# Static attention scores as four quarter-array products of 192 columns, and one PSUM tile per bank

## The chip, the cores and the metric

The kernel runs on one core of a Trainium2 chip. The metric is the device time of one execution in microseconds; a lower time is better. A core has five engines with queues of their own: TensorE (PE; its weight loads are PEld), VectorE (DVE), ScalarE (ACT), GpSimd (POOL) and SyncE (SP), which here only issues DMA transfers. TensorE writes its products to PSUM, eight banks of 512 fp32 columns on 128 partitions; VectorE and ScalarE fetch them from there.

## The reference

Block-sparse attention for 4 batches, 8 heads, 768 positions and a head dimension of 64, and behind it an MLP on the 3072 tokens (width 512, hidden 2048). The mask is by blocks of 32: each query block sees its own and its two neighbours, the first and the last block, and three sampled blocks.

```python
scores = scale * np.matmul(q, k.transpose(0, 1, 3, 2))
mask = np.abs(blk_i - blk_j) <= 1
mask = mask | (blk_i == 0) | (blk_j == 0) | (blk_i == n_blocks - 1) | (blk_j == n_blocks - 1)
for qb in range(n_blocks):
    for kb in sampled_blocks[qb]:
        mask[qb * 32:(qb + 1) * 32, kb * 32:(kb + 1) * 32] = True
scores = np.where(mask, scores, -1000000000.0)
attn = np.exp(scores - np.max(scores, axis=-1, keepdims=True))
attn = attn / (np.sum(attn, axis=-1, keepdims=True) + 1e-09)
x = np.matmul(attn, v)                      # then tokens x 512
h = x @ w_in
r = np.maximum(h, 0.0)
out = (s * (r * r) + b) @ w_out
```

The weights of the MLP come in as float64 and are turned on the chip into two fp32r parts each (high and low).

## The kernel before

**Slots and units.** The attention is a list of slots. A slot of kind s is one batch, one tile of 128 queries and four heads, so four units (one unit is one head's 128 x 352 scores); there are 40. Kind d (dense: the first and the last query block, eight slots of two units with 768 keys each) and kind h (four slots, the queries left over) handle the edges. The query tiles are shifted by one block, so that tile t holds the query blocks 4t+1 to 4t+4.

**One unit's columns.** A unit of kind s has 352 score columns in one bank: 256 static ones (128 of its own chunk of keys, 64 of the first and last block, 64 of the next chunk) and 96 sampled ones. The static scores are one product per head (L710): 64 partitions of head dimension, 128 queries as weights, 256 key columns. Two heads share a call: one sits on array rows 0 to 63, the other on 64 to 127 (`tile_position`). Query blocks 4t+1 and 4t+2 need only columns 0 to 191 of the 256, blocks 4t+3 and 4t+4 only columns 64 to 255; the mask adds a very large negative number to the others. The sampled scores (L736) are 32-query products with gathered keys. Slots d and h (L724) already multiply 64 queries at a time, by four products per call on the four quarters of the array, 384 and 160 columns wide.

**A unit's way.** VectorE adds the mask and takes the maximum (L751, with the scores read from PSUM into an SBUF tile), ScalarE takes the exponential and the row sum (L763), TensorE transposes 3 x 128 columns into another bank (L787), VectorE or ScalarE in turn copies them out (L791, L793), TensorE multiplies with the static values (L832) and the gathered ones (L846). Per slot follow the reciprocal of the sums (L772 to L775), the scaling (L852), a transposition (L858), a copy (L863) and a DMA to DRAM.

**Banks.** `next_bank` goes round seven banks for scores and transposed tiles alike; each call makes a new tile under the bank's tag, which waits until the tile before it under that tag is done. The eighth bank holds the attention's output.

**Order.** No engine's order is left to a scheduler of the compiler. The class `Plan` simulates five queues (TensorE, ScalarE, VectorE, GpSimd, SyncE) with a cost in nanoseconds for each operation (`costs` at L956 for TensorE's, others beside the operation), a priority, and counts of buffers; each engine takes, when free, the operation of best priority that can start first. The order that comes out is the order of the program. TensorE's own order is fixed before that: transposes of slot i, the transposition of slot i-1, the scores of slot i+2, the products with values of slot i. Into the same plan go the decoding of the weights (L75 to L85: six VectorE and three ScalarE operations for each of 32 blocks, with three raw buffers), at a lower priority than the attention, and the first 30 of the 64 steps of the MLP for batches 0 and 1 (`mlp1`, L401 to L403, then ReLU, square, high and low part, `mlp2`, L440 to L442). Behind the plan stand, in an order written out by hand, the rest of those steps and the MLP of batches 2 and 3 (L1193 and on), which uses seven products for eight.

**Limits at the passage.** The hidden tiles have two buffers, their high parts three, and `mlp1` two banks; so `mlp2` of the first step has to run before the fourth step's hidden tile can be finished. `mlp2` of step 0 needs w_out block 0 decoded; the order of decode is w_in blocks 0 to 7, then w_out 0 and so on.

Of the kernel before, what the change touches and what calls it, by code (L numbers as in the profile page):

```python
# [15 lines left out]
ALU = mybir.AluOpType  # L16
# [82 lines left out]
class Plan:  # L99
# [103 lines left out]
def kernel(  # L203
# [16 lines left out]
    nc = tc.nc  # L220
# [3 lines left out]
    D = 64  # L224
# [6 lines left out]
    SC = 256  # L231
# [28 lines left out]
    NBANK = 7  # L260
# [12 lines left out]
    def bank(k, name):  # L273
        return ps.tile([P, 512], F32, tag=f"bank{k}", name=name)
# [184 lines left out]
    with ExitStack() as es:  # L459
# [66 lines left out]
        for t in ptiles:  # L526
            nc.gpsimd.memset(t[:, SW:], 0.0)

        V = nc.vector
        ri = pers.tile([P, 1], I32, name="ri")  # L530
        V.tensor_scalar(out=ri, in0=pi, scalar1=5, scalar2=None, op0=ALU.logical_shift_right)
# [162 lines left out]
        bcount = [0]  # L694

        def next_bank(name):
            bcount[0] += 1
            return bank(bcount[0] % NBANK, name)

        halves = [slice(par * D, (par + 1) * D) for par in range(2)]  # L700

        def scores_static(i, k):


            kind, b, t, x = slots[i]
            n, qr, kt = unit_of[i], qraw[slots[i][:3]], kts[b]
            if kind == "s":
                for par in range(2):
                    sp = sps[(n + 2 * k + par, 0)] = next_bank(f"s{n + 2 * k + par}")
                    nc.tensor.matmul(sp[:, :SC], qr[halves[par], 2 * x + k, :], kt[halves[par], 2 * x + k, 192 * t:192 * t + SC],  # L710
                                     start=True, stop=True, tile_position=(par * D, 0))
                return
            for par in range(2):
                key = (n + par, k) if kind == "d" else (n + 2 * k + par, 0)
                sp = sps[key] = next_bank(f"s{key[0]}_{key[1]}")
                for a in range(2):
                    if kind == "d":
                        o = 64 if k else 0
                        keys = kt[halves[par], 2 * x + a, k * 512:k * 512 + 576].rearrange("p (a c) -> p a c", c=192)[:, :, o:o + P]
                        to, q = sp[halves[a], :HALF], qr[halves[par], 2 * x + a, halves[a]]  # L720
                    else:
                        keys, to = kt[halves[par], 2 * k + a, KW - 6 * BLK:KW - BLK], sp[halves[a], SW - SC:2 * P]
                        q = qr[halves[par], 2 * k + a, halves[a]]
                    nc.tensor.matmul(to, q, keys, start=True, stop=True, tile_position=(par * D, a * D))  # L724
# [41 lines left out]
        def recip(i):  # L766

            kind = slots[i][0]
            nu = 2 if kind == "d" else 4
            dn, rc = dns.pop(i), sm.tile([P, 4], F32, tag="rc", name=f"rc{i}")[:, :nu]  # L770
            if kind == "d":
                nc.vector.scalar_tensor_tensor(out=rc, in0=dn[:, 0, :nu], scalar=1e-9, in1=dn[:, 1, :nu], op0=ALU.add, op1=ALU.add)  # L772
            else:
                nc.vector.tensor_scalar(out=rc, in0=dn[:, 0, :nu], scalar1=1e-9, scalar2=None, op0=ALU.add)
            nc.vector.reciprocal(rc, rc)  # L775
            rcs[i] = rc

        pts_of = {}

# [77 lines left out]
            for pr in range(tr.shape[1]):  # L857
                nc.tensor.transpose(tr[:, pr, :], xv[:, pr * P:(pr + 1) * P], ident)  # L858

        def x_copy(i):  # L860
            tr = tr_of.pop(i)
            xst_of[i] = xp.tile([P, 2, P], F32, tag="xst", name=f"xst{i}", bufs=4)[:, :tr.shape[1], :]
            nc.scalar.copy(xst_of[i], tr)  # L863

        def spill(i):
            kind, b, t, x = slots[i]
# [14 lines left out]
        op = plan.op  # L881
# [71 lines left out]
        pq = pvl = o_m = o_e = o_rc = o_ev = None  # L953
        spills, tensor, lqs = {}, {}, {}

        costs = {"s": (485, 535, 350, 260, 685), "d": (810, 0, 350, 780, 0), "h": (380, 535, 240, 160, 685)}  # L956
        cols = {"s": (1024, 1536, 768, 256, 1024), "d": (1536, 0, 768, 768, 0), "h": (640, 768, 512, 128, 512)}
        for i, (kind, b, t, x) in enumerate(slots):
            u, full, cost, col = unit_of[i], kind == "s", costs[kind], cols[kind]
            nu, ng, nk = (2, 2, 2) if kind == "d" else (4, 1, 2)  # L960
# [29 lines left out]
            for j in range(nu):  # L990
# [7 lines left out]
                for g in range(ng):  # L998
# [9 lines left out]
            o_rc = op("v", 390, u + nu + T["RP"], lambda i=i: recip(i), [o_e], alloc=[("rc", i)], use=[("dn", i)], order=[o_rc])  # L1008

            a_ops = []  # L1010
            for j in range(nu):
# [230 lines left out]
    for i in range(NPL, NSUB):  # L1242
        g, f = subs[i]
# [140 lines left out]
```

## Time and profile before

| | |
|---|---|
| time, median of 3 | 811.12 us (807.78 to 814.91) |
| the profiled execution | 810.37 us; its span 808.6 us, granted clock 0.992 |
| PE busy | 784.5 us (97%) |
| DVE, ACT, POOL busy | 559.1, 494.0, 214.7 us |
| last transposes of the attention | end at 277.8 us |
| bytes | 77.41 MB read, 12.58 MB written |

The span runs from the first to the last instruction of the profiled execution. In rows of groups, "x64 | 9.1, 402 | 0.0" means 64 records, 9.1 us during which at least one ran, 402 ns for one on the mean, and the engine's idle time just before them. A row such as "59.82 1.06 PE s L710 x8" of the chain of waits gives start, length, engine, tile, line and count. In the timeline, "[1.43 <-DVE nm L751]" is idle time before the instruction and what ended it. One fp32 product shows as two MATMUL records. An L with a number is a line of the kernel before.

### The profile page before, as it was taken

What the parts mean: (1) busy time and instruction counts of PE and PEld (TensorE: products, weight loads), DVE (VectorE), ACT (ScalarE), POOL (GpSimd) and SP (SyncE); (2) the same over time, 40 slices, a digit from 0 to 9 for tenths busy, and PEclk for the clock granted to TensorE, in tenths of its full rate; (3) what the DMA queues carried; (4) which work ended last, traced back from release to release, by engine and by line L of the source; (5) the groups of instructions that cost most, each with busy time, mean ns of one, the idle gap of its engine ahead of it and who ended that gap; (6) DMA issues with size and microseconds to landing.
All of it is one profiled execution on the core that took longest, in us unless ns stands there. A gap on an engine that the chain in (4) does not pass through costs nothing.

```text
span 808.6 us, 21993 instructions
## 1 busy us (share of the span) xinstructions
PE 784.5 (97%) x8400; PEld 682.2 (84%) x8400; DVE 559.1 (69%) x1379; ACT 494.0 (61%) x1175; POOL 214.7 (27%) x438
## 2 busy tenths in 40 slices
PE   7899999999998999999999999999999999999997
PEld 6687877888886889999889999998889988899996
DVE  5576778888887899999742222288768869766662
ACT  3576777878787787777663333457445457544542
POOL 5422133222400032222322222223223223322321
PEclk9899999999999999999999999999999999999999
DMA  9999897887777532433221010412200012000002
GB/s 267 248 223 315 231 253 215 244 246 215 220 210 235 144 107 83 130 127 105 86 98 40 27 40 27 150 52 79 86 1 7 0 40 85 16 0 1 1 2 78
DMA packets 86073, 95.61 MB, mean 118 GB/s; under 512 B 11344, under 2 KB 64976, under 8 KB 85968
## 3 DMA queue, kind: packets, MB, share of 16 engines
q1 hardware_dynamic: 85968, 94.21, 39.0%
q8 instruction: 66, 1.08, 0.6%
q14 instruction: 39, 0.32, 0.1%
HBM read 77.41 MB, written 12.58 MB: 111 GB/s over the span
## 4 chain that ended last, share of the span: by engine, by line
PE 84%; DMA 4%; ACT 4%; DVE 3%; issue 3%; SPq 2%; POOL 0%; ACTq 0%; DVEq 0%; POOLq 0%
PE m L1193 13%; PE o L441 10%; PE o L442 10%; PE o L440 10%; PE t L787 8%; PE xs L832 5%; PE s L710 5%; PE h L402 5%; PE h L403 5%; PE h L401 5%; PE xs L846 3%; PE s L736 2%; DMA kt<-in_k_seq_dram 2%; PE s L724 1%; PE xs L821 1%
## 5 line engine op out<-in xcount | busy, mean ns | idle before, releaser
L419 POOL TENSOR_TENSOR hid<-hid,hid 128x384 fp32r<-128x384 f32 x128 | 139.4, 1090 | 438.9 <-ACT hid L415 255.8
L763 ACT ACTIVATE ptile<-ptile,nm 128x352 f32<-128x352 f32 (+2 forms) x208 | 120.8, 584 | 30.5 <-DVE nm L751 29.5
L1210 ACT ACTIVATE hid<-hid,sb_b,sb_s 128x384 f32<-128x384 f32 x64 | 45.3, 708 | 111.9 <-DVE hid L1204 111.8
L410 DVE SCALAR_TENSOR_TENSOR hid<-hid,sb_s 128x384 f32<-128x384 f32 x64 | 40.9, 641 | 89.0 <-ACT hid L406 88.9
L670 POOL COPY kg<-kt 128x128 f32 x264 | 63.6, 294 | 134.9 <-PE s L736 123.9
L751 DVE CUSTOM_DVE_ANT_0 ptile<-s,ms 128x352 f32<-128x352 f32 x160 | 74.3, 521 | 27.8 <-PE s L736 27.5
L401 PE MATMUL h<-x,win 128*128 128x384 f32 x256 | 86.6, 338 | 0.6 <-ACT hid L406 0.6
L402 PE MATMUL h<-x,win 128*128 128x384 f32 x256 | 86.2, 337 | 0.2 <-DVE x L374 0.2
L403 PE MATMUL h<-x,win 128*128 128x384 f32 x256 | 86.4, 337 | 0.0
L787 PE MATMUL t<-ident,ptile 128*128 128x128 f32 x608 | 79.6, 280 | 6.4 <-ACT ptile L763 3.5
L787 PEld LDWEIGHTS t<-ident,ptile 128*128 128x128 f32 x608 | 66.3, 142 | 12.4 <-ACT ptile L763 4.3
L442 PE MATMUL o<-wout,hid 128*128 128x512 f32 x192 | 76.0, 396 | 0.0
L442 PE MATMUL o<-woutr,hid 128*128 128x512 f32 x192 | 76.0, 396 | 0.0
L441 PE MATMUL o<-wout,hid 128*128 128x512 f32 x192 | 75.9, 395 | 0.0
L441 PE MATMUL o<-woutr,hid 128*128 128x512 f32 x192 | 75.8, 395 | 0.0
L440 PE MATMUL o<-wout,hid 128*128 128x512 f32 x192 | 74.8, 389 | 0.0
L440 PE MATMUL o<-woutr,hid 128*128 128x512 f32 x192 | 74.7, 389 | 0.0
L406 ACT ACTIVATE hid<-h 128x384 f32<-128x384 f32 x64 | 31.2, 487 | 54.3 <-PE h L403 52.4
L791 DVE COPY pt<-t 128x384 f32<-128x384 f32 (+1 forms) x104 | 56.1, 545 | 9.9 <-PE t L787 8.0
L414 ACT ACTIVATE hid<-hid,sb_b 128x384 f32<-128x384 f32 x64 | 39.4, 615 | 37.2 <-DVE hid L410 37.2
L1193 PE MATMUL m<-xT,wop 128*128 128x384 f32 x288 | 58.5, 337 | 2.6 <-DVE sum L1286 1.5
L793 ACT COPY pt<-t 128x384 f32<-128x384 f32 (+1 forms) x104 | 48.8, 473 | 15.7 <-PE t L787 14.9
(169 smaller groups left out, 1648.8 us busy)
## 6 DMA issues: line engine op xcount, KB each, us to landing
vg<-in_v_dram SPq DMA_DIRECT2D x136, 128.0 KB, 3.9
v<-in_v_sta_dram SPq DMA_DIRECT2D x40, 256.0 KB, 4.5
kt<-in_k_seq_dram SPq DMA_DIRECT2D x16, 544.0 KB, 8.2
raw_i<-in_w_in_dram SPq DMA_DIRECT2D x16, 512.0 KB, 4.9
raw_o<-in_w_out_dram SPq DMA_DIRECT2D x16, 512.0 KB, 3.2
v<-in_v_dram SPq DMA_DIRECT2D x16, 384.0 KB, 5.4
xd<-xst SPq DMA_DIRECT2D x44, 128.0 KB, 3.9
out_dram<-ob SPq DMA_DIRECT2D x20, 256.0 KB, 2.2
```

Of the source, the lines that this page charges most:

```text
L401: nc.tensor.matmul(ph, wh, xh, start=(c == 0), stop=False)
L402: nc.tensor.matmul(ph, wh, xl, start=False, stop=False)
L403: nc.tensor.matmul(ph, wl, xh, start=False, stop=(c == NCC - 1))
L419: nc.gpsimd.tensor_tensor(out=htile(5 + i % 3), in0=t, in1=gh.bitcast(F32), op=ALU.subtract)
L440: nc.tensor.matmul(acc, gh[:, tsl], wout(f, 0), start=first, stop=False)
L441: nc.tensor.matmul(acc, gh[:, tsl], wout(f, 1), start=False, stop=False)
L442: nc.tensor.matmul(acc, gl[:, tsl], wout(f, 0), start=False, stop=last)
L670: nc.gpsimd.tensor_copy(kg[:, m], kts[b][:, :, bass.ds(box["js"][m], BLK)])
L751: nc.vector.tensor_tensor_reduce(out=pt[:, :w], in0=sps.pop((n, g))[:, :w], in1=msk, scale=-scale, scalar=FMAX if g == 0 else nm[:, 0:1], ...
L763: nc.scalar.activation(pt[:, :w], pt[:, :w], AF.Exp, bias=nms[n][:, last:last + 1], scale=-1.0, accum_out=dns[i][:, g, j:j + 1])
L787: nc.tensor.transpose(tp[:, c, :], src[:, c * P:(c + 1) * P], ident)
L1193: nc.tensor.matmul(to, w_, x_, start=(c == 0 and k == 0), stop=(c == 1 and k == 2))
```

## The change

Three things are edited, the first two for the attention's slots alone.

The static scores of kind s: instead of one product of 128 queries with 256 columns per head, two products of 64 queries with 192 columns, the second shifted by 64 columns. They go to the same places in the bank; 64 of the 256 columns of each half aren't written any more and hold whatever the bank held, to which the mask adds its very large negative number. A call issues four products (two heads, two query halves) where it issued two.

The banks: one tile per bank for the whole attention, set to zero by VectorE at the start (seven memsets of 128 x 512), so that an unwritten place never holds something that isn't a number. The tiles of the MLP are still made anew under the same tags.

The planner's costs: a static call of kind s is set to 410 instead of 485 (and 768 instead of 1024 columns), the last copy of a slot to 300 and 400 instead of 280 and 390. Beside that the sum of the two denominators in slots d takes two operations instead of one, and two helpers are split or get an argument, with the same operations as before.

```diff
+        banks = {}
+        def abank(k):
+            if k not in banks:
+                banks[k] = bank(k, f"abank{k}")
+                nc.vector.memset(banks[k], 0.0)
+            return banks[k]
+        for k in range(NBANK):
+            abank(k)
...
         def next_bank(name):
             bcount[0] += 1
-            return bank(bcount[0] % NBANK, name)
+            return abank(bcount[0] % NBANK)
...
                 for par in range(2):
-                    sp = sps[(n + 2 * k + par, 0)] = next_bank(f"s{n + 2 * k + par}")
-                    nc.tensor.matmul(sp[:, :SC], qr[halves[par], 2 * x + k, :], kt[halves[par], 2 * x + k, 192 * t:192 * t + SC],
-                                     start=True, stop=True, tile_position=(par * D, 0))
+                    sps[(n + 2 * k + par, 0)] = next_bank(f"s{n + 2 * k + par}")
+                for a in range(2):
+                    for par in range(2):
+                        nc.tensor.matmul(sps[(n + 2 * k + par, 0)][halves[a], a * D:a * D + 3 * D], qr[halves[par], 2 * x + k, halves[a]],
+                                         kt[halves[par], 2 * x + k, 192 * t + a * D:192 * t + a * D + 3 * D],
+                                         start=True, stop=True, tile_position=(par * D, a * D))
...
-                nc.vector.scalar_tensor_tensor(out=rc, in0=dn[:, 0, :nu], scalar=1e-9, in1=dn[:, 1, :nu], op0=ALU.add, op1=ALU.add)
+                nc.vector.tensor_scalar(out=rc, in0=dn[:, 0, :nu], scalar1=1e-9, scalar2=None, op0=ALU.add)
+                nc.vector.tensor_tensor(out=rc, in0=rc, in1=dn[:, 1, :nu], op=ALU.add)
...
-        costs = {"s": (485, 535, 350, 260, 685), "d": (810, 0, 350, 780, 0), "h": (380, 535, 240, 160, 685)}
-        cols = {"s": (1024, 1536, 768, 256, 1024), "d": (1536, 0, 768, 768, 0), "h": (640, 768, 512, 128, 512)}
+        costs = {"s": (410, 535, 350, 260, 685), "d": (810, 0, 350, 780, 0), "h": (380, 535, 240, 160, 685)}
+        cols = {"s": (768, 1536, 768, 256, 1024), "d": (1536, 0, 768, 768, 0), "h": (640, 768, 512, 128, 512)}
...
-            ac = op("a", 280 if kind == "d" else 390, u + T["XA"], lambda i=i: x_copy(i), [tr], alloc=[("xst", i)], use=[("o", i)])
+            on = "a"
+            ac = op(on, 300 if kind == "d" else 400, u + T["XA"], lambda i=i, e=on: x_copy(i, e), [tr], alloc=[("xst", i)], use=[("o", i)])
```

More of the change, by code (lines that the diff above doesn't have):

```diff
@@ L764, in exp, with sum_up @@
                                  accum_out=dns[i][:, g, j:j + 1])
-        def recip(i):
+        def sum_up(i):
             kind = slots[i][0]
@@ L771, in recip @@
             if kind == "d":
-                nc.vector.scalar_tensor_tensor(out=rc, in0=dn[:, 0, :nu], scalar=1e-9, in1=dn[:, 1, :nu], op0=ALU.add, op1=ALU.add)
+                nc.vector.tensor_scalar(out=rc, in0=dn[:, 0, :nu], scalar1=1e-9, scalar2=None, op0=ALU.add)
+                nc.vector.tensor_tensor(out=rc, in0=rc, in1=dn[:, 1, :nu], op=ALU.add)
             else:
                 nc.vector.tensor_scalar(out=rc, in0=dn[:, 0, :nu], scalar1=1e-9, scalar2=None, op0=ALU.add)
-            nc.vector.reciprocal(rc, rc)
             rcs[i] = rc
+        def recip(i):
+            nc.vector.reciprocal(rcs[i], rcs[i])
         pts_of = {}
@@ L858, in x_transpose, with x_copy @@
                 nc.tensor.transpose(tr[:, pr, :], xv[:, pr * P:(pr + 1) * P], ident)
-        def x_copy(i):
+        def x_copy(i, eng):
             tr = tr_of.pop(i)
             xst_of[i] = xp.tile([P, 2, P], F32, tag="xst", name=f"xst{i}", bufs=4)[:, :tr.shape[1], :]
-            nc.scalar.copy(xst_of[i], tr)
+            copy_on(eng, xst_of[i], tr)
         def spill(i):
@@ L1007 @@
                     evs.setdefault(j, []).append(o_ev)
-            o_rc = op("v", 390, u + nu + T["RP"], lambda i=i: recip(i), [o_e], alloc=[("rc", i)], use=[("dn", i)], order=[o_rc])
+            o_rc = op("v", 390, u + nu + T["RP"], lambda i=i: (sum_up(i), recip(i)), [o_e], alloc=[("rc", i)], use=[("dn", i)], order=[o_rc])
             a_ops = []
```

## The prediction

> **What bounds the kernel now.** I read the page first (busy shares and the slices), then the chain of waits inside the attention, then busy time by stretch, then the order of time at the end of the attention.
>
> ```profile
> PE 784.5 (97%) x8400; PEld 682.2 (84%) x8400; DVE 559.1 (69%) x1379; ACT 494.0 (61%) x1175; POOL 214.7 (27%) x438
> PE   7899999999998999999999999999999999999997
> DVE  5576778888887899999742222288768869766662
> ```
>
> TensorE is busy in 97% of the span, and no slice after the second falls under 9 tenths but one and the last. VectorE has two faces: 6 to 8 tenths in the attention (slices 3 to 13), 9 in slices 15 to 19, where the MLP has begun and the weights are still being decoded. So the question is not whether TensorE is the bound on the whole, but whether a gain in the attention survives the passage into the MLP.
>
> One slot of the attention, from the chain of waits (start, length, what):
>
> ```profile
> 59.82 1.06 PE s L710 x8
> 60.88 0.49 PE s L736 x32
> 61.37 1.08 PE xs L832 x32
> 62.46 0.58 PE xs L846 x32
> 63.04 1.46 PE t L787 x12
> 64.50 0.22 PE xs L858 x2
> 64.72 1.06 PE s L710 x8
> ```
>
> From one static score (59.82) to the next (64.72) are 4.90 us, and the six TensorE pieces add up to 1.06 + 0.49 + 1.08 + 0.58 + 1.46 + 0.22 = 4.89. The chain is TensorE alone: what a slot saves on TensorE, it saves in time.
>
> ```profile
> 100.00:240.00 140.00, 137.49 (x3324) 112.51 (x3326) 116.78 (x411) 111.58 (x337) 37.69 (x156) 1.00 0.81 229
> 240.00:277.00 37.00, 34.16 (x704) 26.69 (x699) 29.14 (x101) 28.79 (x85) 0.00 (x0) 1.00 0.69 205
> 277.00:296.00 19.00, 18.27 (x144) 17.09 (x143) 18.17 (x34) 14.14 (x27) 3.84 (x3) 1.00 0.29 90
> ```
>
> The columns are PE, PEld, DVE, ACT and POOL busy, then granted clock, DMA share and GB/s. From 100 to 240 us DVE idles 23.2 us and ACT 28.4; from 277 to 296 us DVE idles 0.8 us. That last stretch is VectorE's.
>
> **The static scores.** L710 has five groups of 64 like the first here, 320 records, 8 to a slot: 40 slots of kind s. The second row is another view of one group (duration least, median, most; first and last start).
>
> ```profile
> L710 PE MATMUL s<-kt,qr_1s 64*128 64x256 f32 x64 | 9.1, 402 | 0.0
> L710 PE MATMUL s<-kt,qr_0s x64: 375/376/481, 35.7 to 162.1; 64*128 64x256 f32 x64
> L724 PE MATMUL s<-kt,qr_5h 64*64 64x160 f32 x64 | 3.1, 309 | 0.0
> 118.10 0.70 PE s L724 x16
> 255.68 1.45 PE s L724 x16
> ```
>
> The new form, 64x64 tiles of the array with 192 columns, stands in no row, but its neighbours do: slots h and d run the same four tiles in the same order, with 160 columns (0.70 us for two calls) and 384 columns (1.45 us). Between them lie 0.75 us for 2 x 224 columns, 1.674 ns per column and call. So two calls with 192 columns take 0.70 + 2 x 32 x 1.674 ns = 0.81 us, against 1.06 us now: 0.25 us less per slot, 40 x 0.25 = 10.0 us in all. As for its bounds: streaming alone is 2 x 192 x 1.674 = 0.64 us, and what L710 spends beyond streaming is 1.06 - 2 x 256 x 1.674 = 0.20; with that in place of 0.16 it is 0.84 us, 8.6 us in all. I take 10.0, since its row has the same tiles.
>
> That the four tiles run beside each other is in the row too: 16 records of 309 ns in 0.70 us. [...]
>
> **The start.** Seven memsets of 128x512 on VectorE come ahead of its first work.
>
> ```profile
> 1.99 0.42 POOL L541 MEMSET mz<- 128x384 bf16 x1
> 5.33 0.20 DVE L556 CAST sbf<-sbi 128x72 f32<-128x72 int32 x1 [1.57 <-DMA sbi<-in_sampled_dram]
> 8.17 0.74 DVE L96 SCALAR_TENSOR_TENSOR sbp<-sbf,oner,sbp 128x3 f32<-128x3 f32 x3
> 11.61 0.56 DVE L751 CUSTOM_DVE_ANT_0 ptile<-s,mz 128x384 f32<-128x384 f32 x1 [2.70 <-PE s L724]
> 16.34 0.59 ACT L628 CAST ms<-iv 128x480 bf16<-128x480 f32 x1 [2.64 <-POOL iv L96]
> 16.61 0.55 DVE L791 COPY pt<-t 128x384 f32<-128x384 f32 x1
> ```
>
> No memset of VectorE is in the trace. By POOL's of 384 columns one takes at least 0.42 us, by the copy of 384 columns, scaled to 512, at most 0.73: 2.9 to 5.1 us for seven. VectorE idles some 1.6 us before the cast at 5.33 and 2.7 us before its first maximum at 11.61, so together 4.3 us of it are covered; what is left, under 1 us, goes to a maximum. Queued behind the memsets are the constants and the indices; POOL waits for those, then ACT's mask at 16.34, which the first slot s needs only after its static scores (35.7 us, the first L710). TensorE's first scores wait for the memsets too, but start at 10.6. I book 0; without that cover it would be up to 3 us.
>
> **What else changes.** The sum of denominators in the eight d slots becomes two operations.
>
> ```profile
> 19.82 0.19 DVE L772 SCALAR_TENSOR_TENSOR rc<-dn 128x2 f32<-128x2 f32 x1
> ```
>
> 8 x 0.19 = 1.5 us of VectorE, off the path: 0. One tile per bank asks for the same order of writer and reader on a bank as a fresh tile with the same tag: 0, with a tenth of a us per slot either way as its bound, 4 us, since a wait of that size is under what the rows name. No DMA is added or moved by hand, but SP's order, like every engine's, comes from the planner, and its costs are edited: a static call falls from 485 to 410.
>
> **Where the gain goes.** At the end of the attention:
>
> ```profile
> 247.41 0.43 DVE L75 TENSOR_SCALAR wkhp<-raw_i 128x512 int32<-128x512 int32 x1 [4.03 <-DMA raw_i<-in_w_in_dram]
> 248.76 0.52 PE L787 MATMUL t<-ident,ptile 128*128 128x128 f32 x3 [1.43 <-DVE nm L751]
> 250.34 0.44 PE L858 MATMUL xs<-ident,xss 128*128 128x128 f32 x2 [1.06 <-DVE xss L852]
> ...
> 277.70 0.42 PE L401 MATMUL h<-x,win 128*128 128x384 f32 x1
> 279.29 0.68 DVE L83 TENSOR_TENSOR win<-wkhp,raw_i 128x512 fp32r<-128x512 f32 x1
> 280.01 0.43 DVE L84 TENSOR_SCALAR wkhp<-win 128x512 int32<-128x512 int32 x1
> 280.56 0.68 DVE L85 SCALAR_TENSOR_TENSOR win<-wklp,wkhp 128x512 fp32r<-128x512 f32 x1
> 281.15 0.42 DVE L75 TENSOR_SCALAR wkhp<-raw_i 128x512 int32<-128x512 int32 x1
> 281.49 0.42 DVE L77 TENSOR_SCALAR wklp<-raw_i 128x512 int32<-128x512 int32 x1
> 281.94 0.69 DVE L78 SCALAR_TENSOR_TENSOR wklp<-wklp,raw_i 128x512 f32<-128x512 int32 x1
> ...
> 293.73 0.69 DVE L85 SCALAR_TENSOR_TENSOR wout<-wklp,wkhp 128x512 fp32r<-128x512 f32 x1
> 294.28 0.40 PE L440 MATMUL o<-wout,hid 128*128 128x512 f32 x1
> ```
>
> The second product of the MLP (L440) needs the first decoded block of w_out; that is finished at 293.73 + 0.69 = 294.4, and L440 starts at 294.28. TensorE fills the 16.6 us from 277.70 with first products (L401 to L403), and by the code it can't make many more: the hidden tile of the fourth waits for the first L440, and behind it there are two banks for products. VectorE meanwhile finishes the last w_in blocks that the order puts ahead, then w_out 0, with 0.8 us of pause. So both meet at 294.3, and if the attention ends 10.0 us earlier, the first L440 comes earlier only by as much as VectorE gets the decode done earlier.
>
> Decode has the lowest rank in the attention and fills the gaps that the planner sees. In the planner's own units a slot s has on VectorE 4 x 600 + 2 x 560 + 390 + 430 = 4340, on TensorE 2 x 485 + 535 + 4 x 350 + 4 x 260 + 685 + 230 = 4860; with 410 it is 4710. The gap falls from 520 to 370, on ScalarE (4490, then 4500) from 370 to 210. The stretch with decode in it, and the static scores alone from 100 to 240 us:
>
> ```profile
> 103.62 0.51 SPq L57 DMA_DIRECT2D raw_i<-in_w_in_dram  x1
> 100.00:240.00 140.00, 28.37 (x200) 17.23 (x200) 1.00 0.81 229
> ```
>
> Weight loads run from 104 us, and 200 records of L710 are 25 slots. So 25 x 150 = 3750 units less room on VectorE, at 3470 a block (its six operations in the planner's cost) 1.1 blocks; on ScalarE 25 x 160 = 4000 at 2010 a block, 2.0 blocks. Blocks not done in the attention are done behind it, where VectorE has no gap: a block is 0.42 + 0.42 + 0.69 + 0.68 + 0.43 + 0.68 = 3.3 us by the rows. Lost again: 1.1 x 3.3 = 3.6 to 2.0 x 3.3 = 6.6 us, if the planner fills its room wholly; that it doesn't (23 us of DVE idle) speaks for the lower part, 4.5 us. The bounds are 0 (rival 1) and all of it (rival 2). After 300 us TensorE runs without a gap and every later stage only shifts.
>
> **The sum.** -10.0 (scores) + 4.5 (decode left over) + 0 (start) + 0 (the rest) = -5.5 us. The profiled execution took 810.4 us (span 808.6 and 1.8 around it), the median is 811.1, so the time is 811.1 - 5.5 = 805.6, 0.7%. One per cent, 8.1 us, is about what a measurement of this kernel tells from no change.
>
> **Rivals.** (1) *The decode keeps its pace*: real VectorE has 23 us idle against 6 us (25 x 0.25) that go, so the same operations fit in shorter slots. Then the passage moves whole: 811.1 - 10.0 = 801; without the stall of 1.43 + 1.06 us at 248 us, which hangs on the order, 798.6. Chance 0.28. (2) *The decode eats it all*: three blocks left over, 3 x 3.3 = 9.9: 811. Chance 0.13. (3) *Slower*: the weight stream itself slips, since all decode goes through three raw buffers and VectorE's queue in order; a decode step put ahead of its data holds the maxima behind it, as at 247.41 (4.03 us of VectorE, 2.5 us of TensorE). From 3.0 blocks left over the change loses; with five it is 811.1 - 10.0 + 16.5 = 817.6. For it: the order is made anew and the margin at L440 is nil. Against it: no other stall of that size stands in the chain but
>
> ```profile
> 136.55 2.90 DMA vg<-in_v_dram
> ```
>
> Chance 0.12. (4) *More instructions cost their issue*: L736 issues 32 records in 0.49 us, 15 ns each; 8 more at that price are 0.12 us per slot, the saving 0.13, 5 us in all, with 4.5 lost behind: 810.6. Chance 0.05; the 0.70 us row speaks against it. [...] The forecast itself: 0.42, its own range 802 to 809.
>
> **How the numbers follow.** Faster by over 1% (under 803.0): nearly all of (1), 0.26, and the lower edge of the forecast, 0.06: 0.32. Slower by over 1% (over 819.2): the far half of (3), 0.07. Within: 0.61. The range goes from (1) without its stall, 798, to most of (3), 816.
>
> **What would show it.** Right: the chain's slot shrinks to 4.65 us, "PE s L710"'s successor reads 0.81 us with 16 records; the first L401 comes near 268 us; the first L440 stands at 288 to 290 us with some 4 us of TensorE idle before it; after that equal lengths. Rival 1: L440 at 284. Wrong: a score piece above 0.9 us, new waits for DMA in the attention, or an L440 at or behind 294 us.

## The result, and the profile after

| | before | after |
|---|---|---|
| time, median (lowest to highest) | 811.35 us (807.75 to 814.91) | 817.49 us (812.91 to 820.25) |
| ratio after to before | | 1.0071, 95% interval 1.0047 to 1.0095 |
| the profiled execution | 810.37, its span 808.6 | 816.87, its span 814.9 |

The change made the kernel slower, by 6 us where 5.5 us of gain was forecast. In the rows of after, the static scores are L726, the products of slots d and h L741, the sampled scores L753, the maxima L768, the exponential L780, the transposes L807, the products with values L852 and L866 (d: L841), the scaling L872, a slot's last transposition L878, its transfer to DRAM (the spill) L895, the gathers of values L665. The MLP's lines are unchanged up to L446.

The page of after, busy time and slices:

```profile
PE 781.2 (96%) x8720; PEld 678.8 (83%) x8720; DVE 560.9 (69%) x1394; ACT 494.4 (61%) x1175; POOL 216.8 (27%) x438
PE   6899997999999979999999999999999999999997
PEclk9999998999999979999999999999999999999999
```

TensorE works 3.3 us less and the span is 6.3 us longer. Two slices have fallen to 7, the seventh (122 to 143 us) and the fifteenth (285 to 306 us), and the granted clock has fallen with them. One slot in the chain of waits of after:

```profile
91.74 1.46 PE abank L807 x12
93.21 0.22 PE xs L878 x2
93.42 0.81 PE abank L726 x16
94.23 0.49 PE abank L753 x32
94.73 1.08 PE xs L852 x32
95.81 0.58 PE xs L866 x32
96.39 1.46 PE abank L807 x12
```

The score piece is 0.81 us with 16 records and the slot 96.39 - 91.74 = 4.65 us, both as forecast. So the time was lost between slots like this one. The start of the last transposition of some slots (L858 before, L878 after; slots are counted from 0), in us, shows where:

| slot | 17 | 21 | 22 | 51 (the last) | end of the span |
|---|---|---|---|---|---|
| before | 117.7 | 135.0 | 141.4 | 281.3 | 808.6 |
| after | 111.6 | 130.7 | 142.9 | 279.1 | 814.9 |
| after less before | -6.1 | -4.3 | +1.5 | -2.2 | +6.3 |

There are two losses: 5.8 us between slots 21 and 22, and 8.5 us between the end of the attention and the MLP's steady part. The lead of 6.1 us at slot 17 is not the products' alone: after leads by 1.0 us at slot 3 and by 3.8 at slot 15, which is 0.23 us for each slot between; then slot 16 takes 6.6 us in before, where slot 15 took 4.9.

**The first loss: gathered values.** The long transfers in the chain of after, with the transposes behind the third; the order of time of TensorE at that place; and busy time by stretch (PE, PEld, DVE, ACT, POOL, granted clock, DMA share, GB/s):

```profile
35.09 6.44 DMA v<-in_v_dram
...
82.36 4.06 DMA vg<-in_v_dram
...
136.56 2.70 DMA vg<-in_v_dram
...
140.38 2.75 PE abank L807 x12
...
221.90 3.69 DMA vg<-in_v_dram
```

```profile
136.16 0.35 PE L866 MATMUL xs<-vg,pt 96*32 96x64 f32 x2 [2.47 <-DMA vg<-in_v_dram]
137.56 0.39 PE L866 MATMUL xs<-vg,pt 96*32 96x64 f32 x2 [1.05 <-DMA vg<-in_v_dram]
139.35 1.03 PE L866 MATMUL xs<-vg,pt 96*32 96x64 f32 x26 [1.39 <-DMA vg<-in_v_dram]
```

```profile
135.00:140.00 5.00, 1.40 (x29) 1.01 (x30) 0.00 (x0) 0.14 (x2) 0.00 (x0) 0.62 0.80 231
140.00:145.00 5.00, 5.00 (x86) 4.22 (x79) 2.56 (x9) 1.60 (x5) 0.08 (x1) 0.70 0.90 238
```

Of the four, only the one at 136 us stands in the chain of before. TensorE's waits for gathered values from 30 to 285 us (sum, times, longest), before and after, are

```profile
PE xs L846 <- DMA vg<-in_v_dram: 0.9, 2, 0.6
PE xs L866 <- DMA vg<-in_v_dram: 5.8, 4, 2.5
```

The gather for slot 22 ends its chain at 136.56 + 2.70 = 139.26 us. Before, the same piece was 136.55 + 2.90 = 139.45. TensorE reached slot 22's sampled products (L866) 4.6 us earlier, at 133.4 instead of 138.0 us, and the data came at the same moment. On top of that comes the clock: in the five microseconds of the stall TensorE is busy 1.40 us at a mean granted clock of 0.62. The clock is 1.00 up to 136.2 us, where the gap of 2.47 us ends, and 0.50 from there to 143.0 us, so the twelve transposes behind the stall take 2.75 us instead of 1.46.

**The second loss: the passage.** From after's order of time, and the stretches behind (the low part of a weight block is made by L85, its high part by L83):

```profile
294.81 0.50 PE L440 MATMUL o<-wout,hid 128*128 128x512 f32 x1 [1.46 <-DVE wout L83]
295.99 0.50 PE L441 MATMUL o<-wout,hid 128*128 128x512 f32 x1 [0.68 <-DVE wout L85]
...
297.34 0.63 PE L442 MATMUL o<-wout,hid 128*128 128x512 f32 x1
...
301.14 0.69 PE L401 MATMUL h<-x,win 128*128 128x384 f32 x1 [1.89 <-ACT hid L406]
```

```profile
295.00:300.00 5.00, 3.57 (x9) 2.06 (x8) 2.94 (x7) 2.88 (x6) 0.44 (x1) 0.66 0.28 107
300.00:305.00 5.00, 3.86 (x11) 3.48 (x12) 4.82 (x8) 2.26 (x5) 0.56 (x1) 0.50 0.33 112
```

The first L440 stands at 294.81 us, behind VectorE's decode of w_out. There are three waits of 1.46, 0.68 and 1.89 us within 8 us, and the granted clock of the stretches falls to 0.66 and 0.50; a product of 512 columns takes 0.63 instead of 0.40 us. Of the 8.5 us, 2.7 are lost up to the first L440 (294.28 us before, 294.81 in after, with an attention that ended 2.2 us earlier) and 5.8 behind it. At the first loss the clock was at one half (0.50, the least that any half microsecond of before or after shows) right behind the gap of 2.47 us; here it was so from 296.6 to 306.8 us, behind the gaps of 1.46 and 0.68 us and already ahead of that of 1.89.

### The profile page after: what moved, and what is told of

It is laid out like the page before. It is cut to its first block, busy times and chain, and to the rows that moved or that the text cites. A ratio compares the mean times of both kernels' runs of the same rounds, so it can differ in the third digit from the quotient of the medians.

```text
span 814.9 us, 22664 instructions
## 1 busy us (share of the span) xinstructions
PE 781.2 (96%) x8720; PEld 678.8 (83%) x8720; DVE 560.9 (69%) x1394; ACT 494.4 (61%) x1175; POOL 216.8 (27%) x438
## 4 chain that ended last, share of the span: by engine, by line
PE 81%; DMA 5%; DVE 4%; ACT 4%; issue 3%; SPq 2%; POOL 1%; ACTq 0%; DVEq 0%; POOLq 0%
PE m L1214 13%; PE o L441 10%; PE o L442 10%; PE o L440 10%; PE abank L807 8%; PE xs L852 5%; PE h L401 4%; PE h L402 4%; PE h L403 4%; PE abank L726 3%; PE xs L866 3%; PE abank L753 2%; DMA kt<-in_k_seq_dram 2%; DMA vg<-in_v_dram 1%; PE abank L741 1%
## 5 line engine op out<-in xcount | busy, mean ns | idle before, releaser
L780 ACT ACTIVATE ptile<-ptile,nm 128x352 f32<-128x352 f32 (+2 forms) x208 | 120.8, 583 | 22.6 <-DVE nm L768 22.3
L768 DVE CUSTOM_DVE_ANT_0 ptile<-abank,ms 128x352 f32<-128x352 f32 x160 | 74.3, 521 | 26.0 <-PE abank L753 25.8
L401 PE MATMUL h<-x,win 128*128 128x384 f32 x256 | 87.0, 340 | 2.1 <-ACT hid L406 2.1
L807 PE MATMUL abank<-ident,ptile 128*128 128x128 f32 x608 | 80.3, 283 | 3.5 <-ACT ptile L780 3.5
L441 PE MATMUL o<-wout,hid 128*128 128x512 f32 x192 | 77.1, 401 | 0.7 <-DVE wout L85 0.7
L440 PE MATMUL o<-wout,hid 128*128 128x512 f32 x192 | 75.9, 395 | 1.5 <-DVE wout L83 1.5
L442 PE MATMUL o<-wout,hid 128*128 128x512 f32 x192 | 77.0, 401 | 0.0
L441 PE MATMUL o<-woutr,hid 128*128 128x512 f32 x192 | 75.8, 395 | 0.0
L807 PEld LDWEIGHTS abank<-ident,ptile 128*128 128x128 f32 x608 | 67.2, 143 | 9.1 <-ACT ptile L780 4.4
L440 PE MATMUL o<-woutr,hid 128*128 128x512 f32 x192 | 74.6, 389 | 0.0
L811 DVE COPY pt<-abank 128x384 f32<-128x384 f32 (+1 forms) x104 | 56.2, 545 | 9.9 <-PE abank L807 3.2
L813 ACT COPY pt<-abank 128x384 f32<-128x384 f32 (+1 forms) x104 | 48.5, 474 | 15.0 <-PE abank L807 14.5
```

Source lines behind the costliest of these rows:

```text
L401: nc.tensor.matmul(ph, wh, xh, start=(c == 0), stop=False)
L440: nc.tensor.matmul(acc, gh[:, tsl], wout(f, 0), start=first, stop=False)
L441: nc.tensor.matmul(acc, gh[:, tsl], wout(f, 1), start=False, stop=False)
L442: nc.tensor.matmul(acc, gl[:, tsl], wout(f, 0), start=False, stop=last)
L768: nc.vector.tensor_tensor_reduce(out=pt[:, :w], in0=sps.pop((n, g))[:, :w], in1=msk, scale=-scale, scalar=FMAX if g == 0 else nm[:, 0:1], ...
L807: nc.tensor.transpose(tp[:, c, :], src[:, c * P:(c + 1) * P], ident)
```

## The experiments

The two theories at first were: **A**, the planner's new costs make a new order in which the decode comes late, and the order of before with half tiles would be fast; **B**, the half tiles themselves gain nothing, whatever the order.

### The order and the products apart

e1 is after with the old costs, so half tiles in the old order:

```diff
-        costs = {"s": (410, 535, 350, 260, 685), "d": (810, 0, 350, 780, 0), "h": (380, 535, 240, 160, 685)}
-        cols = {"s": (768, 1536, 768, 256, 1024), ...
+        costs = {"s": (485, 535, 350, 260, 685), "d": (810, 0, 350, 780, 0), "h": (380, 535, 240, 160, 685)}
+        cols = {"s": (1024, 1536, 768, 256, 1024), ...
...
-            ac = op(on, 300 if kind == "d" else 400, ...
+            ac = op(on, 280 if kind == "d" else 390, ...
```

> The changed kernel (four products, one tile per bank, memsets) with the planner's costs of the kernel before, so that every engine works in the order of before. Theory A (the new order loses what the products gain: SyncE's queue brings the gather of slot 22 too late, decode is two blocks behind at the passage): the score pieces read 0.81 us, no stall of several us at the gather, the first L440 comes earlier than 294 us: 803 to 808 us. Rival B (shorter slots collide with the transfers and the decode in any order): 812 us or more, again with stalls over 2 us at the gather and low granted clock behind them.

e2 is before with the three lines the other way round:

> The kernel before (two products, a fresh tile per use of a bank) with the planner's new costs alone, so that every engine works in the order of after. Theory A: the order alone does harm at the passage, where fewer blocks are decoded, and none at the gather, which is reached later: 815 to 819 us. Rival B: the order is neutral, 809 to 813 us, and only the shorter slots hurt.

e3 is before with one tile per bank and the seven memsets, as in the change's own diff:

> The kernel before with one tile per bank and the seven memsets alone. Both theories: 811 us within 2; the memsets take 2.9 to 5.1 us of VectorE at the start, of which under 2 us reach the first slot. A rival in which one tile per bank adds waits on the banks would give 0.1 us per slot and more, 815 us.

e4 is after with w_out's first blocks earlier in the order of decode:

```diff
-    "WL": "i0 i1 i2 i3 i4 i5 i6 i7 o0 o1 o2 o3 o4 o5 o6 i8 ...
+    "WL": "i0 i1 i2 i3 i4 o0 o1 i5 o2 i6 o3 i7 o4 o5 o6 i8 ...
```

> The changed kernel with another order of decode: w_out blocks 0 and 1 ahead of w_in block 5, and so on in turn. Theory A (the passage waits for w_out 0 and 1, and the clock falls behind the wait): w_out 0 is done before the seven first products are, no wait at the first L440, granted clock 1.0 through the passage: 809 us within 3. Rival C (VectorE's total of decode is the limit, whichever block comes first): another block is late instead, 815 to 819 us.

| | median, us | ratio to before (95%) | slot 21 | slot 22 | slot 51 | span |
|---|---|---|---|---|---|---|
| e1, half tiles, old order | 814.74 | 1.0017 (0.9984 to 1.0051) | 135.3 | 145.7 | 288.1 | 815.4 |
| e2, old tiles, new order | 817.59 | 1.0061 (1.0027 to 1.0095) | 131.6 | 144.0 | 282.5 | 816.9 |
| e3, old tiles, bank tiles | 810.71 | 0.9973 (0.9941 to 1.0004) | 134.6 | 142.7 | 282.1 | 809.3 |
| e4, after, w_out earlier | 814.50 | 1.0028 (0.9996 to 1.0060) | 134.2 | 144.3 | 281.3 | 811.3 |

The tiles by bank cost nothing that can be measured (e3). The new costs alone cost as much as the whole change (e2), and in e2 the passage looks like after's:

```profile
298.23 0.50 PE L440 MATMUL o<-wout,hid 128*128 128x512 f32 x1 [1.48 <-DVE wout L83]
...
303.79 0.45 PE L401 MATMUL h<-x,win 128*128 128x384 f32 x1 [2.25 <-ACT hid L406]
```

In e1 the passage is clean again:

```profile
284.52 0.42 PE L401 MATMUL h<-x,win 128*128 128x384 f32 x1
...
301.08 0.40 PE L440 MATMUL o<-wout,hid 128*128 128x512 f32 x1
```

From the first L401 to the first L440 are 301.08 - 284.52 = 16.56 us without a wait for the decode; before it was 294.28 - 277.70 = 16.58. By 240 us five blocks of weights are wholly decoded (five records of L85) in before and in e1, and four in after and in e2. So in the old order VectorE's decode moves with the attention, and the second loss belongs to the new order. The table says the same: from slot 51 to the end of the span are 527.3 us in before, 527.3 in e1 and 527.2 in e3, but 535.8 in after and 534.4 in e2. e4, with 530.0 us, gets part of it back: its first L440 follows the first L401 after 8.5 us, at 288.70, with no wait. But its expectation's rival C, that another block comes late instead, is partly true. It still loses 2.7 us against before, and loses them late: its 65th L440 starts at 377.3 us (before 377.6), its 101st at 428.9 (before 426.2). Among the waits between are two for the decode of a later block of w_out, 0.52 us at 402.4 and, here as a row of waits, 0.7 us at 403.5:

```profile
PE o L441 <- DVE woutr L85: 0.7, 1, 0.7
```

And neither is fast: e1 stands at 814.7 where theory A had 803 to 808, and e4 got back 3 of the 8 us that A gave it. e1's attention ends 6.8 us later than before's, though every undisturbed slot is 0.25 us shorter. Theory A named one half of the loss; the other was open.

### What holds the values back

In every one of these kernels the gather for slot 22 landed between 139 and 142 us, whether its buffer had come free at 120 or at 126 us. SyncE's order of time, before:

```profile
127.54 0.55 SPq L514 DMA_DIRECT2D v<-in_v_sta_dram  x1
129.13 1.97 SPq L653 DMA_DIRECT2D vg<-in_v_dram  x3
131.53 0.35 SPq L875 DMA_DIRECT2D xd<-xst  x1
132.08 4.79 SPq L653 DMA_DIRECT2D vg<-in_v_dram  x9
```

and after:

```profile
119.97 1.96 SPq L895 DMA_DIRECT2D xd<-xst  x1
...
128.62 2.98 SPq L665 DMA_DIRECT2D vg<-in_v_dram  x4
131.70 0.37 SPq L895 DMA_DIRECT2D xd<-xst  x1
132.26 4.61 SPq L665 DMA_DIRECT2D vg<-in_v_dram  x8
```

The buffer came free 5.2 us earlier in after (120.3 instead of 125.5 us), but SyncE began with the gather only 0.5 us earlier: it was still working through the transfers ahead of it, and took 8 us more for the twelve of the gather. Two theories: **Q**, SyncE's queue, in order and full, holds the gathers back; **B** from here on, the rate of the transfers does (some 240 GB/s, transfer engines busy 85% of the time from 100 to 140 us). The spill seemed the cheapest thing to move, since SyncE waited 30 us for ScalarE there between 60 and 280 us.

```diff
-            nc.sync.dma_start(out=to, in_=xst)
+            nc.scalar.dma_start(out=to, in_=xst)
```

This was put into after (e5), e1 (e6), before (e7) and e4 (e11):

> The changed kernel with the 52 transfers of finished tiles to DRAM (the spill) issued from ScalarE's queue instead of SyncE's; everything else as changed. In the changed kernel SyncE waits some 3.4 us for ScalarE's copies between 100 and 140 us, and the gather of the values for slot 22 is first issued at 128.6 us though its buffer came free at 120.3, and lands at 139.3 us. Theory Q (SyncE's queue, which works in order, holds the gather back): it is issued 3 to 5 us earlier and lands near 135, the wait of TensorE before slot 22's sampled products falls from about 5 us to under 1, the end of the attention moves 3 to 6 us forward, and with the passage as bad as in the changed kernel the time is 811 to 814. Theory B (the transfers themselves, 240 GB/s in that stretch, are the limit): the gather lands at 138 to 142 as in every run so far and the time is 815 to 819.

> The changed kernel with the planner's costs of before and the spill on ScalarE's queue: half-tile products, tiles by bank, the old order, and SyncE without its waits for ScalarE. The same without the queue change took 814.7 us. Theory Q: the stalls for gathered and static values in the attention shrink from some 10 us to 2 to 4, the products' 0.25 us per slot become time, and the kernel takes 803 to 809. Theory B: 813 to 817, with the gather for slot 22 still landing at 139 to 142 us.

> The kernel before with only the spill moved to ScalarE's queue. Its slots need the gathered values 4.6 us later than those of the changed kernel, and they came 1 us late. Both theories: 809 to 812, since there is about 1 us of such waiting to win; under theory Q the gather for slot 22 lands at 134 to 137 us, under theory B at 138 to 142. If this kernel gains as much as the two with half tiles, the queue has nothing to do with the change.

> The changed kernel with the first two blocks of w_out decoded before the last three early blocks of w_in (814.5 us on its own) and the spill on ScalarE's queue. Theory Q: the two losses, at the gather of slot 22 and at the passage, are separate and add up, so 807 to 811, under the kernel before. Theory B: 813 to 816, as without the queue change.

Measured were 852.96, 856.72, 855.94 and 844.55 us, ratios of 1.041 to 1.057 (intervals from 1.037 to 1.061): all four 4 to 6% slower, which no theory had. SyncE's waits from 60 to 280 us in e6 show what was new (sum, times, longest):

```profile
SPq L665 <- DMA xd<-xst: 29.1, 14, 6.5
SPq L500 <- DMA xd<-xst: 15.7, 6, 5.0
SPq L514 <- DMA xd<-xst: 12.5, 6, 3.3
```

SyncE now waits 57 us for the spills' landing before it issues gathers, queries and values (61 us by the same three rows in e5 and in e11). That wait is new; it did not stand in after. So the move put a longer wait in place of a shorter one. It tells Q from B only weakly, yet it points at Q: from 100 to 140 us the transfer engines were busy 0.73 of the time in e6 and moved 199 GB/s, less than before, and the attention was 44 us longer.

The next try leaves the spill on SyncE and puts it a slot later into the plan:

```diff
-            spills[i] = op("s", 450, u + T["SPP"], lambda i=i: spill(i), [ac], ...
+            if i:
+                spill_op(*held, ac)
+            held = i, u, ac, kind
```

> The changed kernel with the spill of each slot put a slot later into the plan (issued by SyncE again, but planned behind the copy of the following slot), so that SyncE reaches it when ScalarE has long made the copy. Between 60 and 280 us SyncE waited some 30 us for ScalarE at the spill in the changed kernel. The planner then also gives a slightly different order of decode and copies. Theory Q (SyncE's queue in order holds the gathers and values back): the waits of the spill shrink from 30 us to under 8, the gather for slot 22 lands 3 to 6 us earlier than at 139.3, the end of the attention moves from 279.1 to about 273 to 276, and with the passage as bad as before 811 to 814. Theory B (the transfers' own rate): landing at 138 to 142 as ever, 815 to 819.

> Half tiles and a tile for each bank with the planner's costs of before (814.7 us by itself), and the spill a slot later in the plan: TensorE's, VectorE's and ScalarE's orders are those of that kernel and only SyncE's differs. Theory Q: 804 to 809, the gather for slot 22 landed by 137 us and the waits for values in the attention under 5 us in all. Theory B: 813 to 817.

> The kernel before with the spill a slot later in the plan; again only SyncE's order differs. Theory Q: the gather for slot 22 lands earlier here too, but this kernel waited only about 1 us for it, so 808 to 811: the difference between this kernel and the same with half tiles is then 2 to 6 us in favour of the half tiles. Theory B: 810 to 812 and no difference in favour of the half tiles.

> The changed kernel with w_out's first two blocks decoded earlier (814.5 us by itself) and the spill a slot later in the plan; TensorE's order is that of the former. Theory Q: both losses mended, 804 to 809. Theory B: 813 to 816.

Measured: e13 816.22 us (ratio 1.0088, 1.0053 to 1.0123), e14 817.63 (1.0083, 1.0054 to 1.0112), e15 811.99 (1.0020, 0.9993 to 1.0047), e16 812.66 (1.0025, 0.9995 to 1.0055). Nothing moved, and the gather for slot 22 landed at 139.9, 144.3, 139.0 and 142.1 us. SyncE's largest wait in after from 60 to 280 us, and in e13:

```profile
SPq L895 <- ACT xst L813: 18.0, 10, 4.0
```

```profile
SPq L508 <- PE xs L852: 14.2, 4, 4.9
```

The wait for ScalarE's copy fell from 18.0 to 0.6 us, and others came in its place: all of SyncE's waits there sum to 76 us in after and to 72 in e13. By these runs Q in its narrow form, the spill's wait, was wrong; they don't say whether SyncE would still be late with fewer waits in all.

### Bytes or issues

The last two sets separate the transfers' size from their number. Theory B says that the bytes set the pace; the theory called Q, and then I, that SyncE's issuing of so many transfers in order does. Each set keeps the orders of TensorE, VectorE and ScalarE and halves the gathered bytes, and so leaves half of the sampled part out of the output. The first keeps all 136 gathers and halves the width of each:

```diff
-                nc.sync.dma_start(out=vg[k * BLK:(k + 1) * BLK, :, r, :], in_=src)
+                nc.sync.dma_start(out=vg[k * BLK:(k + 1) * BLK, :, r, :DM // 2], in_=src[:, :, :DM // 2])
```

> The kernel before with the same number of gathers of values (136 issues) but each brings only the first half of the columns (64 KB instead of 128 KB); the other half of the two gather buffers is set to zero once, so half of the sampled part of the output is left out. Orders of TensorE, VectorE and ScalarE are those of the kernel before. Some 7 MB fewer of the 50 MB between 60 and 280 us. Theory B (the rate of the transfers paces the first half of the attention): little to win here, since this kernel waits about 1 us for the gather of slot 22 and a few for others: 804 to 809; the gather for slot 22 lands by 134 us. Theory Q (SyncE's order and issue are the limit, not the bytes): landing stays at 138 to 142 and the time at 809 to 812.

> The changed kernel with half-width gathers (half of the sampled part of the output left out). Theory B: the gather for slot 22 lands some 6 us earlier, the half-tile products' 0.25 us per slot become time, the attention ends 5 to 8 us earlier than at 279.1 us, and what is left against the kernel before with half-width gathers is the loss at the passage: 807 to 812. Theory Q: 815 to 819, as the changed kernel.

> Half tiles and a tile for each bank in the order of before (814.7 us by itself), with half-width gathers (half of the sampled part of the output left out). Theory B: 5 to 9 us under the kernel before with half-width gathers, so 797 to 803: with values in time the products give what they save. Theory Q: 813 to 817.

> The changed kernel with w_out's first blocks decoded earlier (814.5 us by itself), with half-width gathers (half of the sampled part of the output left out). Theory B: 800 to 806, both losses gone. Theory Q: 812 to 816.

The second keeps the width and leaves every second gather out:

```diff
+                if r % 2:
+                    return
```

> The kernel before with every second gather of values left out (68 issues instead of 136, each of the full 128 KB; the rows that are not gathered are set to zero once, so half of the sampled part of the output is left out). The bytes are those of the half-width gathers, the issues on SyncE are half as many. Orders of TensorE, VectorE and ScalarE as before. Theory I (SyncE's issuing, some 0.55 us for each transfer and in order, sets the pace): the gather for slot 22 lands 3 us and more earlier than the 136.2 us of the half-width gathers, at 133 or before; the time is 803 to 807, little under the 807.7 of the half-width gathers, since the kernel before hardly waits there. Theory B (bytes): landing at 136 and 806 to 809.

> Half tiles and a tile for each bank in the order of before, with every second gather of values left out (half of the sampled part of the output is left out). Theory I: the gather for slot 22 lands by 132 us, the waits for gathered values vanish, and the half tiles give 5 to 9 us against the kernel before with the same gathers: 795 to 801. Theory B: as with the half-width gathers, 808 to 811, 2 us over the kernel before with the same gathers.

| | median, us | ratio to before (95%) | gather for slot 22 landed | slot 51 | span |
|---|---|---|---|---|---|
| e17, before, half width | 807.73 | 0.9944 (0.9911 to 0.9977) | 136.2 | 276.4 | 803.5 |
| e18, after, half width | 812.54 | 0.9999 (0.9964 to 1.0034) | 137.0 | 275.4 | 812.2 |
| e19, half tiles in the old order, half width | 809.97 | 0.9955 (0.9924 to 0.9986) | 137.6 | 279.5 | 806.7 |
| e20, e4 with half width | 809.14 | 0.9946 (0.9909 to 0.9983) | 139.5 | 281.3 | 812.4 |
| e21, before, half the gathers | 799.60 | 0.9893 (0.9842 to 0.9944) | 127.5 | 270.4 | 797.6 |
| e22, half tiles in the old order, half the gathers | 794.33 | 0.9808 (0.9762 to 0.9855) | 125.6 | 262.1 | 789.4 |

Half the bytes moved the landing by 1 to 4 us, and only the time of e17 came out where theory B had it; e18 missed its range by 0.5 us, e19 and e20 met neither theory, and against e17 the half tiles in the old order (e19) still gained nothing. Half the issues moved it by 12 to 16 us, further than theory I had asked, and both times came out lower than it had said. SyncE and the stretch from 100 to 140 us in e19, half tiles with half-width gathers:

```profile
127.69 2.21 SPq L670 DMA_DIRECT2D vg<-in_v_dram  x3
130.01 0.38 SPq L900 DMA_DIRECT2D xd<-xst  x1
130.88 5.03 SPq L670 DMA_DIRECT2D vg<-in_v_dram  x9
```

```profile
100.00:140.00 40.00, 34.56 (x868) 27.65 (x857) 28.38 (x104) 28.07 (x87) 13.69 (x56) 0.95 0.73 207
```

and in e22, the same kernel and bytes with half the gathers:

```profile
118.92 2.22 SPq L672 DMA_DIRECT2D vg<-in_v_dram  x3
121.24 0.37 SPq L902 DMA_DIRECT2D xd<-xst  x1
121.85 1.32 SPq L672 DMA_DIRECT2D vg<-in_v_dram  x3
```

```profile
100.00:140.00 40.00, 39.70 (x1089) 32.42 (x1082) 34.64 (x126) 34.40 (x106) 14.46 (x60) 1.00 0.80 217
```

In e19 nine gathers of half the width still take 5.03 us to issue, 0.56 us each on the mean, as the whole ones did (4.79 for nine before, 0.53 each): in both rows one gather starts 0.50 us behind the other, but for one step of about 1 us. Meanwhile the transfer engines idle 27% of the time. In e22 SyncE is at the gather 8.8 us earlier, within 2 us of the buffer's release (117.2 us), and TensorE is busy 39.70 of 40 us at full clock. From 30 to 285 us TensorE no longer waits for gathered values in e22, against 4.2 us in e19. So what held the values back is above all the number of transfers that SyncE issues in order, its own time for each and the waits between them, and their bytes far less; how much of it is SyncE's own time and how much the waits was not separated.

With the values in time, the half tiles pay (e22 has the tiles by bank as well, whose cost e3 could not tell from nothing). In the medians e22 is 799.60 - 794.33 = 5.3 us under e21, in the profiled spans 8.2, of 10.0 that the products save; the two intervals against before overlap by little. And the passage in e22:

```profile
258.57 0.42 PE L401 MATMUL h<-x,win 128*128 128x384 f32 x1
...
275.12 0.40 PE L440 MATMUL o<-wout,hid 128*128 128x512 f32 x1
```

is again 16.55 us long and without a wait for the decode, though the attention ends 19 us earlier than before's. From slot 51 to the end of the span e17, e19, e21 and e22, all in the old order, take 527.1 to 527.3 us, and e18, in the new one, 536.8. No kernel that does the whole work beat the kernel before: e3 is the lowest, and its interval includes 1.

## Why the prediction was wrong

**The score piece** was right: 0.81 us with 16 records, 4.65 us for a slot. The trace agrees with the sum from the rows of slots d and h: beyond 1.674 ns for each column and call the 16 records cost 0.81 - 2 x 192 x 1.674 ns = 0.17 us, about the 0.70 - 2 x 160 x 1.674 ns = 0.16 us of the 16 records of a slot h.

**"What a slot saves on TensorE, it saves in time"** is the step that failed first. It was read from one slot at 60 us, whose chain was TensorE alone. The row "136.55 2.90 DMA vg" in the prediction was taken only as the size of a rare stall, for rival 3. It was the end of a SyncE queue that had no time left: before already waited 0.9 us there, so any lead that TensorE won before slot 22 had to be given back. Measured: a lead of 6.1 us at slot 17, a lag of 1.5 at slot 22, and a lead of 2.2 us at the end of the attention where 10.0 was booked. With half the issues the term is 8.2 us in the profiled spans and 5.3 in the medians (e22 against e21). "New waits for DMA in the attention" stood among the prediction's own signs of being wrong.

**Decode left over, +4.5 us**, had the right place, direction and cause: the gaps that the planner sees, which the edit of its costs makes shorter. e2 shows that the costs do it with the old products too, and in the old order (e1, e22), where real slots are as short, the passage does not change by 0.1 us: that is rival 1. One block fewer was decoded by 240 us, where the sum had 1.1 to 2.0. Up to the first L440 the term was 2.7 us, less than the 4.5 that was booked; the L440 itself came at 294.81 and not at 288 to 290, since the attention ended only 2.2 us earlier.

**"After 300 us TensorE runs without a gap and every later stage only shifts"** is the second step that failed. The sum had nothing for what follows the first L440, and there 5.8 us were lost: further waits of 0.68 and 1.89 us, and a granted clock of 0.50 from 296.6 to 306.8 us. They hang on the same decode: in e4, with w_out's first blocks earlier, the clock is 1.00 all through the passage (285 to 310 us). From 317 us on, where the 17th L440 of after starts 6.3 us behind before's, the rest only shifts, as the prediction has it. One reading was off as well. The prediction has L440 wait for the whole block of w_out; in after's rows L440 waits for L83, the high part, and L441 for L85, the low part. In before it is L441 that had no margin, since L85 ended at 294.42 us:

```profile
294.52 0.46 PE L441 MATMUL o<-wout,hid 128*128 128x512 f32 x1
```

**The start, 0 us.** The memsets:

```profile
0.93 3.73 DVE L535 MEMSET abank<- 128x512 f32 x7 [0.93 <-PEq L1394]
```

3.73 us lie within the 2.9 to 5.1 of the prediction. The first slot's last transposition is 1.7 us later in after and 0.8 in e3, and by the second slot both are ahead of before, so no loss of the memsets is left to see. Each of the seven lasts 485 ns, between the 0.42 and the 0.73 us that the prediction took as its bounds.

**One tile per bank, 0 us**, was right within what e3 can tell (0.9941 to 1.0004).

**The rivals.** Rival 3 gave nearly the time that was measured, 817.6, but by another mechanism: decode fell back by one block and not by five, and the rest was the gathered values and the waits and low clock behind the first L440. Rival 4 falls with the score piece. The sum, by the measured terms of the profiled execution: 4.3 us of lead up to slot 21, 5.8 lost at slot 22, 3.7 won again until the end of the attention (so -2.2 us), then 8.5 lost at the passage (2.7 up to the first L440, 5.8 behind it): +6.3 us.

## What to carry to other kernels

A saving on the busiest engine is worth, at each place, no more than the slack of what feeds it there; look for the rows where the engine waits for data even a little, and ask what sets that moment, before multiplying a saving by its count. A queue that issues in order can be full while the transfer engines are not (in e19 nine gathers of 64 KB took SyncE 5.03 us, and the transfer engines idled 27% of the time from 100 to 140 us): count its transfers and their issue time, not only the bytes. And an edit of a planner's costs is a change of its own; time it without the products it is meant for.

## What the runs showed of the hardware that was not expected

Nine gathers of values in a row take SyncE 4.79 us when each moves 128 KB and 5.03 us when each moves 64 KB: 0.32 us for the issuing instruction of most, 0.50 us from one start to the next, and one longer step. The twelve for slot 22 took before 7.7 us, from 129.13 to 136.87 us, while a single one landed 2.4 to 4.5 us behind its issue. Their number weighed more than their bytes: half as many gathers were worth 11 us to the kernel before (799.60 against 810.89), half the bytes in as many gathers 4 us (807.73 against 811.87).

In after the granted clock stood at one half for longer than the waits ahead of it: 0.50 for 6.8 us behind a gap of 2.47 us, with waits of 1.05 and 1.39 us within them, and for 10.2 us behind 1.46 and 0.68 us in a row, with a wait of 1.89 us within them. It does not always come so: in e2 nearly the same two gaps, 1.48 and 0.69 us, left it at 1.00 up to 305 us, and the stretch from 305 to 310 us, behind the 2.25 us that followed, shows 0.66. What decides it, these runs do not settle.

Issuing one kind of transfer from another engine added 57 us of SyncE's waiting for those transfers to land in e6, 61 in e5 and in e11, and made all four kernels 4 to 6% slower.
